# Preparing part of the second layer's weight factors inside that layer, and sending their stores through another engine's queue

## The chip, the cores and the metric

One core of one Trainium2 chip. The metric is the device time of one execution of the program in microseconds (us); the kernel before took 1364.68 us, the median of 3 runs (1362.75 to 1365.15). TensorE is called PE, VectorE DVE, ScalarE ACT, GpSimd POOL and SyncE SP, as in the profile.

## The reference

Softmax attention in chunks of 64 tokens, then a gated layer, then a mixture of four experts, all in float32:

```python
x = attention(q, k, v)                      # 2304 tokens x 512
x = ((x @ w_a) * (x @ w_b)) @ w_out         # 512 -> 1536 -> 512
p = probs / (probs.sum(-1) + 1e-9)
for e in range(4):                          # w1: 512 x 1024, w2: 1024 x 512
    out += p[:, e] * (relu(x @ w1[e]) @ w2[e])
```

## The kernel before, in words

A product of float32 matrices is made of three reduced-precision ones: each factor is cut into a high part (a cast on ACT, `split_hi`, L96) and a low part (the rest, a subtraction on DVE, L103, or on POOL, L111). PE multiplies high by high, high by low and low by high.

**Order of the work.** Everything is in a hand-written schedule: each engine's and each DMA queue's instructions run in the order in which the program issues them. The 2304 tokens are five blocks; block 0 has 256 tokens, the others 512. First the attention is interleaved with the first two slices of the gated layer (the loop over `spans` from L1035, rounds r = 0 to 10); then the loop over F from L1063 does the rest of the gated layer, block by block (`j`; "A" stands for blocks 1 and 2 in one, done in seven products in place of eight). Together this is called the first layer here. From L1155 on comes the mixture, called the second layer: 16 pairs of weight slices g, for blocks 1 and 2 in a first pass (a = 0 to 15) and for blocks 3 and 4 in a second pass (a = 16 to 31), again by seven products. Step s of the loop at L1164 interleaves seven part steps i: the up product of pair a = s (`a_steps`, L619) and the down product of pair o = s - 1 (`o_step`, L850). Block 0 is too small for that and goes along in plain products, `a0_step` (L459 to L461) and `o0_step` (L924), in the steps that `blk0` picks: pairs 0 to 7 in the first pass, pairs 8 to 15 in the second.

**The factors of the second layer.** The seven products need sums of quarters of the weights as well as the quarters. `prep_ahead` makes them: for each of 32 halves n of a pair, a raw tile is loaded (L194, SP's queue); `ent` splits the first two factors out of it (k = 0, 1), `sums` replaces its quarters by sums with four DVE instructions (L103, `raw<-raw`), and `ent` splits the other two (k = 2, 3). Each finished factor, 512 KB of high and low part, is stored to DRAM by `save` (L176, SP's queue, `kept<-w`) and loaded again by `load_l2` (L241, SP's queue, `w<-kept`) when the second layer needs it, once for each pass. That is 32 loads, 128 factors and 128 stores, in a list `ahead` of 160 entries, of which each call of `prep` runs the next one. Before the change the low parts go to POOL and DVE in turn:

```python
t = split_w(half, eng=(nc.gpsimd, nc.vector)[made[0] % 2])
unsaved.append(((g, 4 * i + k), t))
save(1)
```

All 160 entries are run in the first layer: in rounds r > 3 behind every odd step, and later behind six steps of a block and nine of "A".

**Buffers.** A factor's tile comes from the pool `w` (9 tiles), which also holds the first layer's own split weights; a tile is given again when its last reader is done, which for a factor is its store. Raw tiles come from the pool `raw` (4 tiles), which also takes the first layer's weights as they are loaded (L133). In the first layer ACT also casts the gated product (`gh`, L96) whose low part POOL makes (`ag`, L111); both go into PE's next product (L459 to L461). In the second layer ACT and POOL split the up product's results (`hB`) and their differences (`hT`, L830 and L111), which PE reads in the down product.

Of the kernel before, what the change touches and what calls it, by code (L numbers as in the profile page):

```python
# [8 lines left out]
F32 = mybir.dt.float32  # L9
F32R = mybir.dt.float32r  # L10
# [7 lines left out]
P = 128  # L18
# [10 lines left out]
def fused_kernel(  # L29
# [25 lines left out]
    nc = tc.nc  # L55
# [5 lines left out]
    NG2 = w2p.shape[0]  # L61
# [11 lines left out]
    raw_p = ctx.enter_context(tc.tile_pool(name="raw", bufs=4))  # L73
# [9 lines left out]
    late = {}  # L83
# [76 lines left out]
    def w_tile():  # L160
        return w_p.tile([P, 2, 512], F32R, tag="w", name="w")

    def split_w(src, t=None, eng=nc.gpsimd):
        t = w_tile() if t is None else t
        split_hi(t[:, 0, :], src)
        sub_hi(eng, t[:, 1, :], src, t[:, 0, :])
        return t

    saved = {}
    unsaved = []  # L170

    def save(behind=0):
        while len(unsaved) > behind:
            key, t = unsaved.pop(0)
            saved[key] = tc.dram_tile([P, 2, 512], F32, name="kept" + "_".join(map(str, key)))
            nc.sync.dma_start(out=saved[key], in_=t.bitcast(F32))  # L176

    PAIRS = (
        (("A11", "A12"), ("A22", "A21"), ("S2", "S4"), ("S1", "S3")),
        (("A11", "A21"), ("A12", "A22"), ("S2", "S3"), ("S4", "S1")),  # L180
    )
    made = [0]

    def prep_ahead():

        raw2 = {}
        todo = [(g, i) for g in range(NG2) for i in range(2)]

        def load(n):
            if n < len(todo):  # L190
                g, i = todo[n]
                r = raw2[n] = raw_p.tile([P, 1024], F32, tag="raw", name="raw2")
                src = w2p[g, :, 2 * i : 2 * i + 2, :]
                nc.sync.dma_start(out=r, in_=src.rearrange("p a n -> p (a n)"))  # L194

        def ent(n, k):
            g, i = todo[n]
            if n == 0 and k == 0:
                load(0)
            if k == 0:  # L200
                load(n + 1)
            half = raw2[n][:, 512 * (k % 2) :][:, :512]
            made[0] += 1
            t = split_w(half, eng=(nc.gpsimd, nc.vector)[made[0] % 2])
            unsaved.append(((g, 4 * i + k), t))
            save(1)

        def sums(n):
            q = [raw2[n][:, 256 * x : 256 * x + 256] for x in range(4)]
            a11, a12, a22, a21 = q if todo[n][1] == 0 else (q[0], q[2], q[3], q[1])  # L210
            add_sb(a22, a21, a22)
            add_sb(a21, a11, a21, ALU.subtract)
            add_sb(a11, a22, a11, ALU.subtract)
            add_sb(a12, a12, a11, ALU.subtract)

        for n in range(len(todo)):
            yield from (lambda n=n, k=k: ent(n, k) for k in range(2))
            yield lambda n=n: sums(n)
            yield from (lambda n=n, k=k: ent(n, k) for k in (2, 3))

    ahead = list(prep_ahead())

    def prep(n=1):
# [744 lines left out]
    with tc.manual_schedule():  # L968
# [66 lines left out]
        for r, (f, j, i0, nt) in enumerate(spans):  # L1035
            steps = list(ab_steps(f, j, i0, nt))
            for i, go in enumerate(x2):
                steps.insert(2 * i + 2, go)
            fs = (f,) if j < 3 else (0, 1)
            x2 = x2_steps(fs, j, i0, nt) if f or j < 3 else []  # L1040
            slots = slots_by[r] - slot_no[0]
            done = 0
            for i, step in enumerate(steps):
                while done < slots and done * len(steps) <= i * slots:
                    attn_slot()
                    done += 1
                step()
                if done == slots:
                    x_lo_rest()
                if r > 3 and i % 2:  # L1050
                    prep()
                for go in T.get((r, i), ()):
                    go()
            if r == 3:
                domain_probs()
            if r == 9:
                probs_rows()
            if r == 8:
                early.close()
                late["mid"] = mid.enter_context(tc.tile_pool(name="mid", bufs=1, side="right"))  # L1060


        for F in range(1, NP1):  # L1063
            T = {}
            end = F == NP1 - 1
# [20 lines left out]
            if not end:  # L1086
                n = F + 1
# [26 lines left out]
            for j in ("A", 3, 4, 0) if end else (1, 2, 3, 4, 0) if F == 1 else (4, "A", 3, 0):  # L1114
                if j == "A":
                    steps = seq_ab(F)
                    after = [4, 5, 6, 7]
                else:
                    nt = blocks[j][1]
                    s0, s1 = (list(ab_steps(f, j, 0, nt)) for f in (2 * F, 2 * F + 1))  # L1120
                    steps = s0[:4] + s1[:4] + s0[4:] + s1[4:]
                    if len(x2) > 4:
                        after = [6 + i for i in range(8)]
                    elif j == 0:
                        after = [8 + 2 * i for i in range(4)]
                    elif F > 1 and j == 4 and not end:
                        after = [8 + i for i in range(4)]
                    elif j == 1:
                        after = [4 + i for i in range(4)]
                    else:  # L1130
                        after = [5 + i for i in range(4)]
                if end and j == 3:
                    place = dict(B11="s1", B21="s2", T3="s3", T2="s4", T1="s5", T4="s6", B22="s7")
                    for (u, s), go in zip(at, in_turn(in_place(acc[1], acc[2])), strict=True):
                        put(u, s, go)
                for s, step in enumerate(steps):
                    step()
                    for i, go in enumerate(x2):
                        if after[i] == s:
                            go()  # L1140
                    if s in ((0, 1, 2, 3, 4, 5, 6, 7, 8) if j == "A" else (1, 2, 3, 4, 6, 8)):
                        prep()
                    if end and j == 0 and s == 2:
                        assert not ahead
                        save()
                        load_l2(3)
                    for go in T.get((j, s), ()):
                        go()
                fs = (2 * F, 2 * F + 1)
                x2 = [x for i in ((1, 2) if j == "A" else (j,)) for x in x2_steps(fs, i, 0, blocks[i][1])]  # L1150
                if end and j == "A":
                    mid.close()
                    late["1"] = ctx.enter_context(tc.tile_pool(name="late1", bufs=1, side="right"))


        last = 2 * NG2 - 1
# [2 lines left out]
        tmp = []  # L1159

        def blk0(a):
            return 0 <= a <= last and (a < NG2) == (a % NG2 < NG2 // 2)

        for s in range(last + 2):  # L1164
            a, o = s, s - 1
# [50 lines left out]
            for i in range(7):  # L1216
                if a <= last:
                    steps[i]()
                if s == 0 and i in (2, 3):
                    for go in x2[2 * i - 4 : 2 * i - 2]:  # L1220
                        go()
                    if i == 3:
                        first.close()
                        late["2"] = ctx.enter_context(tc.tile_pool(name="late2", bufs=1))
                        late["ps"] = ctx.enter_context(
                            tc.tile_pool(name="po", bufs=2, space=bass.MemoryType.PSUM)
                        )
                if o >= 0:
                    o_step(o, order[i], True if o == last and i == 6 else None)
                    if i < len(ts):  # L1230
                        ts[i]()
                    if o == last:
                        if i == 2:
                            e[0]()
                        if i == 3:
                            e[1]()
                        if i == 4:
                            e[2]()
                            e[3]()
                        if i == 5:  # L1240
                            e[4]()
                            e[6]()
                            e[5]()
                        if i == 6:
                            out_dma(1, "A22", 1, 0)
                for go in more.get(i, ()):
                    go()
                if i == 2 and o >= 0 and blk0(o):
                    o0_step(o)
                if s and i in (2, 5) and blk0(a):  # L1250
                    a0_step(a, i // 3)
                if s == 0 and i == 6:
                    a0_step(0, 0)
                    a0_step(0, 1)
                load_l2(take[i])


_OUTS = [((2304, 512), "float32")]
# [60 lines left out]
```

## Time and profile before

| | us |
|---|---|
| three runs, median (lowest, highest) | 1364.68 (1362.75, 1365.15) |
| the profiled execution's own time | 1359.91 |
| its span, first to last instruction | 1358.1 |
| PE, DVE, POOL, ACT busy in it | 1246.6, 994.0, 805.3, 431.4 |
| mean granted clock of PE | 0.964 |

The span is what the profile covers. Busy is the time in which an engine had at least one instruction of the program running; an idle engine is only of interest where it holds up the one that sets the pace. The granted clock is a share of PE's full speed of 2.4 GHz; at every moment it is at one of two levels, 2.4 or 1.2 GHz, so a mean of 0.92 is a mixture of the two.

### The profile page before, as it was taken

What the parts mean: (1) busy time and instruction counts of PE and PEld (TensorE: products, weight loads), DVE (VectorE), ACT (ScalarE), POOL (GpSimd) and SP (SyncE); (2) the same over time, 40 slices, a digit from 0 to 9 for tenths busy, and PEclk for the clock granted to TensorE, in tenths of its full rate; (3) what the DMA queues carried; (4) which work ended last, traced back from release to release, by engine and by line L of the source; (5) the groups of instructions that cost most, each with busy time, mean ns of one, the idle gap of its engine ahead of it and who ended that gap; (6) DMA issues with size and microseconds to landing.
All of it is one profiled execution on the core that took longest, in us unless ns stands there. A gap on an engine that the chain in (4) does not pass through costs nothing.

```text
span 1358.1 us, 18139 instructions
## 1 busy us (share of the span) xinstructions
PE 1246.6 (92%) x6676; PEld 1018.1 (75%) x6676; DVE 994.0 (73%) x1311; ACT 431.4 (32%) x785; POOL 805.3 (59%) x605
## 2 busy tenths in 40 slices
PE   8986869879889898799999999999999999999996
PEld 5865657667767677688888888887778888888884
DVE  7866457887678776855477677787887787767668
ACT  4643352433343443323421222222342222222211
POOL 4533356665455664635655556779988776655553
PEclk9988888889999999899999999999999999999999
DMA  7675565465465754425455456766567765645452
GB/s 276 213 266 179 188 196 203 159 217 192 165 247 171 234 199 155 171 78 176 153 179 190 157 184 207 231 222 216 194 217 256 244 226 190 200 154 175 167 170 78
DMA packets 76819, 261.34 MB, mean 192 GB/s; under 512 B 8546, under 2 KB 8618, under 8 KB 76732
## 3 DMA queue, kind: packets, MB, share of 16 engines
q1 hardware_dynamic: 76732, 260.19, 56.9%
q8 instruction: 53, 0.87, 0.3%
q14 instruction: 34, 0.28, 0.1%
HBM read 188.29 MB, written 71.86 MB: 192 GB/s over the span
## 4 chain that ended last, share of the span: by engine, by line
PE 56%; DVE 6%; POOL 6%; DMA 3%; issue 3%; ACT 1%; SPq 0%; DVEq 0%; POOLq 0%; ACTq 0%
PE pm L619 22%; PE po L850 20%; PE po L924 3%; PE pm L506 3%; DMA kept<-w 3%; DVE raw L103 2%; POOL hT L111 1%; PE ps L459 1%; PE ps L460 1%; PE ps L461 1%; PE pm L461 1%; PE pm L460 1%; PE pm L459 1%; POOL w L111 1%; POOL hB L111 1%
## 5 line engine op out<-in xcount | busy, mean ns | idle before, releaser
L99 DVE TENSOR_TENSOR y<-po,y 128x1024 f32<-128x1024 f32 x209 | 255.1, 1220 | 94.1 <-PE po L850 94.1
L850 PE MATMUL po<-hT,w 128*128 128x512 f32 x768 | 197.6, 391 | 9.8 <-POOL hT L111 7.4
L619 PE MATMUL pm<-cT,w 128*128 128x512 f32 x768 | 195.9, 390 | 0.0
L619 PE MATMUL pm<-cB,w 128*128 128x512 f32 x672 | 176.6, 399 | 18.6 <-ACT ag L644 18.6
L850 PEld LDWEIGHTS po<-hT,w 128*128 128x128 f32 x768 | 143.2, 188 | 43.9 <-POOL hT L111 11.5
L619 PEld LDWEIGHTS pm<-cT,w 128*128 128x128 f32 x768 | 143.1, 188 | 30.0
L619 PEld LDWEIGHTS pm<-cB,w 128*128 128x128 f32 x672 | 127.0, 192 | 47.4 <-ACT ag L644 20.6
L850 PE MATMUL po<-hB,w 128*128 128x512 f32 x576 | 149.1, 395 | 0.0
L506 PE MATMUL pm<-xh,w 128*128 128x512 f32 (+1 forms) x576 | 141.6, 368 | 2.9 <-DVE ag L99 2.9
L111 POOL TENSOR_TENSOR w<-raw,w 128x512 fp32r<-128x512 f32 x64 | 89.7, 1402 | 86.8 <-ACT w L96 82.9
L459 PE MATMUL ps<-ag,w 128*128 128x512 f32 (+1 forms) x244 | 97.1, 398 | 43.1 <-POOL ag L111 33.5
L850 PEld LDWEIGHTS po<-hB,w 128*128 128x128 f32 x576 | 108.5, 189 | 25.1 <-DVE y L99 0.4
L111 POOL TENSOR_TENSOR ag<-ag,gh 128x512 fp32r<-128x512 f32 (+1 forms) x61 | 77.1, 1268 | 81.1 <-ACT gh L96 73.6
L96 ACT CAST w<-raw 128x512 fp32r<-128x512 f32 x128 | 77.4, 619 | 143.4 <-DMA kept<-w 69.3
L506 PEld LDWEIGHTS pm<-xh,w 128*128 128x128 f32 x576 | 103.6, 197 | 21.4 <-issue 3.3
L103 DVE SCALAR_TENSOR_TENSOR raw<-raw 128x256 f32<-128x256 f32 x128 | 76.3, 596 | 55.3 <-POOL w L111 52.0
L103 DVE SCALAR_TENSOR_TENSOR w<-raw,w 128x512 fp32r<-128x512 f32 x64 | 60.5, 947 | 63.7 <-ACT w L96 62.3
L154 POOL TENSOR_TENSOR t<-t,raw 128x512 int32<-128x512 int32 x36 | 48.0, 1333 | 83.4 <-DVE t L146 26.4
L461 PE MATMUL ps<-gh,w 128*128 128x512 f32 (+1 forms) x244 | 93.6, 384 | 1.1 <-POOL w L111 1.1
L460 PE MATMUL ps<-gh,w 128*128 128x512 f32 (+1 forms) x244 | 93.9, 385 | 0.0
L111 POOL TENSOR_TENSOR hT<-u,hT 128x512 fp32r<-128x512 f32 x64 | 93.4, 1459 | 0.1
L459 PEld LDWEIGHTS ps<-ag,w 128*128 128x128 f32 x244 | 48.7, 199 | 59.5 <-POOL ag L111 39.8
(140 smaller groups left out, 2358.1 us busy)
## 6 DMA issues: line engine op xcount, KB each, us to landing
w<-kept SPq DMA_DIRECT2D x256, 512.0 KB, 4.2
kept<-w SPq DMA_DIRECT2D x128, 512.0 KB, 5.2
raw<-in_w1p_dram SPq DMA_DIRECT2D x36, 512.0 KB, 4.3
raw<-in_w2p_dram SPq DMA_DIRECT2D x32, 512.0 KB, 4.8
q<-in_q_dram SPq DMA_DIRECT2D x18, 256.0 KB, 4.1
k<-in_k_dram SPq DMA_DIRECT2D x18, 256.0 KB, 4.4
v<-in_v_dram SPq DMA_DIRECT2D x18, 256.0 KB, 5.2
pb<-probs_n SPq DMA_DIRECT2D x8, 512.0 KB, 6.9
```

What stands on the lines that cost most here:

```text
L96: nc.scalar.copy(out=dst, in_=src)
L99: nc.vector.tensor_tensor(out=out, in0=in0, in1=in1, op=op)
L103: nc.vector.scalar_tensor_tensor(out=out, in0=in0, scalar=1.0, in1=in1, op0=ALU.mult, op1=op)
L111: eng.tensor_tensor(out=dst, in0=src, in1=hi.bitcast(F32), op=ALU.subtract)
L154: nc.gpsimd.tensor_tensor(out=t.bitcast(I32), in0=t.bitcast(I32), in1=low.bitcast(I32), op=ALU.add)
L459: nc.tensor.matmul(out=ps[:, :n], lhsT=wh, rhs=al, start=(m == 0), stop=False)
L460: nc.tensor.matmul(out=ps[:, :n], lhsT=wh, rhs=ah, start=False, stop=False)
L461: nc.tensor.matmul(out=ps[:, :n], lhsT=wl, rhs=ah, start=False, stop=(m == last))
L506: nc.tensor.matmul(out=st[i][:, :n], lhsT=x, rhs=y, start=m == 0, stop=m == 3 * KD - 1)
L619: nc.tensor.matmul(out=ps, lhsT=x, rhs=y, start=first and kk == 0 and m == 0, stop=kk == 1 and m == 2, skip_group_check=not first,)
L850: nc.tensor.matmul(out=ps[:, d, :], lhsT=x[:, s], rhs=y, start=m == 0, stop=m == 2)
L924: nc.tensor.matmul(out=ps[:, k, :], lhsT=x[:, f, s], rhs=y, start=f == 0 and m == 0, stop=f == 1 and m == 2,)
```

## The change

Stores go out on ACT's queue; low parts are always made on POOL; the order in `prep_ahead` is such that a half's sums stand behind the last two factors of the half before; `prep` is called less often in the first layer and, new, in the second layer's steps s >= 1 at i = 0, 1, 3, 4 and 6, where a factor's tile comes from the pool `raw`; and block 0 goes along in all 16 steps of the first pass and in none of the second.

```diff
-            nc.sync.dma_start(out=saved[key], in_=t.bitcast(F32))
+            nc.scalar.dma_start(out=saved[key], in_=t.bitcast(F32))
...
         def ent(n, k):
             g, i = todo[n]
-            if n == 0 and k == 0:
-                load(0)
-            if k == 0:
-                load(n + 1)
+            save()
             half = raw2[n][:, 512 * (k % 2) :][:, :512]
-            made[0] += 1
-            t = split_w(half, eng=(nc.gpsimd, nc.vector)[made[0] % 2])
+            t = None
+            if "2" in late:
+                t = raw_p.tile([P, 2, 512], F32R, tag="raw", name="made")
+            t = split_w(half, t)
             unsaved.append(((g, 4 * i + k), t))
-            save(1)
+            if k == 3:
+                load(n + 2)
...
-        for n in range(len(todo)):
-            yield from (lambda n=n, k=k: ent(n, k) for k in range(2))
-            yield lambda n=n: sums(n)
-            yield from (lambda n=n, k=k: ent(n, k) for k in (2, 3))
+        yield lambda: (load(0), load(1))
+        for n in range(len(todo) + 1):
+            if n < len(todo):
+                yield from (lambda n=n, k=k: ent(n, k) for k in range(2))
+            if n:
+                yield from (lambda n=n, k=k: ent(n - 1, k) for k in (2, 3))
+            if n < len(todo):
+                yield lambda n=n: sums(n)
...
-                if r > 3 and i % 2:
+                if r > 4 and i % 8 in (1, 4, 6):
                     prep()
...
-                    if s in ((0, 1, 2, 3, 4, 5, 6, 7, 8) if j == "A" else (1, 2, 3, 4, 6, 8)):
+                    if s in ((0, 2, 4, 6, 8, 10) if j == "A" else (1, 3, 6, 9)) and not (end and j == 0):
                         prep()
                     if end and j == 0 and s == 2:
-                        assert not ahead
                         save()
                         load_l2(3)
...
         def blk0(a):
-            return 0 <= a <= last and (a < NG2) == (a % NG2 < NG2 // 2)
+            return 0 <= a < NG2
...
+                if s and i not in (2, 5):
+                    prep()
                 if i == 2 and o >= 0 and blk0(o):
                     o0_step(o)
...
                 load_l2(take[i])
+            if not ahead:
+                save()
```

## Rows read from the trace of the kernel before

**Rows 1.** Windows: us, busy us (and instructions) of PE, PEld, DVE, ACT, POOL; clock; DMA.

```profile
74.00:581.00 507.00, 424.25 (x2124) 340.11 (x2123) 363.60 (x553) 202.37 (x370) 274.21 (x202) 0.92 0.57 194
...
400.00:450.00 50.00, 47.99 (x220) 39.35 (x219) 38.58 (x56) 18.13 (x33) 27.02 (x20) 0.97 0.55 182
350.00:400.00 50.00, 43.87 (x214) 36.49 (x214) 35.04 (x58) 21.51 (x40) 29.43 (x23) 0.95 0.59 209
...
625.00:821.00 196.00, 196.00 (x961) 165.54 (x961) 129.38 (x153) 49.36 (x90) 111.73 (x89) 1.00 0.53 177
...
925.00:1025.00 100.00, 92.49 (x387) 72.82 (x387) 85.01 (x79) 35.27 (x51) 92.26 (x57) 0.98 0.64 215
1025.00:1142.00 117.00, 117.00 (x514) 96.19 (x514) 92.21 (x98) 27.22 (x48) 88.44 (x68) 1.00 0.71 234
```

**Rows 2.** Waits of PE, 74 to 581 us: total us, times, longest us.

```profile
PE ps L459 <- POOL ag L111: 32.4, 15, 7.4
PE pm L619 <- ACT ag L644: 18.6, 4, 6.4
```

**Rows 3.** The chain that ended last, 336 to 581 us: shares of it by line.

```profile
by line: DMA kept<-w 15.6%; issue 12.3%; PE pm L619 9.8%; DVE raw L103 8.7%; PE pm L506 6.9%; POOL w L111 5.1%; DVE xacc L99 4.0%; PE ps L459 3.7%; PE ps L460 3.6%; PE ps L461 3.5%; ACT w L96 3.5%; DVE t L143 2.8%; DVE w L103 2.5%; POOL t L
```

**Rows 4.** Waits of SP's queue, of ACT and of DVE, 74 to 581 us.

```profile
SPq L176 <- DVE w L103: 140.4, 31, 13.5
...
SPq L176 <- POOL w L111: 48.7, 20, 6.6
...
ACT w L96 <- DMA kept<-w: 81.0, 29, 8.3
ACT w L96 <- DVE raw L103: 37.5, 11, 4.6
...
DVE raw L103 <- POOL w L111: 52.0, 22, 6.0
```

**Rows 5.** Groups of instructions, 74 to 581 us: busy us, mean ns, idle before.

```profile
L111 POOL TENSOR_TENSOR w<-raw,w 128x512 fp32r<-128x512 f32 x64 | 89.7, 1402 | 86.8 <-ACT w L96 82.9 <-DVE s L103 2.1 <-PE ps L461 1.8
L96 ACT CAST w<-raw 128x512 fp32r<-128x512 f32 x128 | 77.4, 619 | 143.4 <-DMA kept<-w 69.3 <-DVE raw L103 37.5 <-issue 21.8
L103 DVE SCALAR_TENSOR_TENSOR raw<-raw 128x256 f32<-128x256 f32 x128 | 76.3, 596 | 55.3 <-POOL w L111 52.0
L103 DVE SCALAR_TENSOR_TENSOR w<-raw,w 128x512 fp32r<-128x512 f32 x64 | 60.5, 947 | 63.7 <-ACT w L96 62.3 <-DMA kept<-w 1.3
```

**Rows 6.** Tile views of raw and kept: ns min/median/max; landing in us.

```profile
L103 DVE SCALAR_TENSOR_TENSOR w<-raw,w x64: 674/693/1805, 74.9 to 578.1; 128x512 fp32r<-128x512 f32 x64
L111 POOL TENSOR_TENSOR w<-raw,w x64: 1258/1294/2369, 75.4 to 579.3; 128x512 fp32r<-128x512 f32 x64
...
L176 SPq DMA_DIRECT2D kept<-w x128: 319/382/1330, 75.6 to 581.0; - x128
...
DMA to landing us min/median/max: 2.6/4.4/8.4
```

**Rows 7.** Timeline of the second layer: POOL's low parts and PE's first use.

```profile
742.39 1.29 POOL L111 TENSOR_TENSOR hT<-g,hT 128x512 fp32r<-128x512 f32 x1
...
753.26 1.52 PE L850 MATMUL po<-hT,w 128*128 128x512 f32 x6
...
759.58 1.30 POOL L111 TENSOR_TENSOR hT<-u,hT 128x512 fp32r<-128x512 f32 x1
...
762.88 1.52 PE L850 MATMUL po<-hT,w 128*128 128x512 f32 x6
```

**Rows 8.** Timeline, DVE: once a step, with block 0, then two steps without.

```profile
746.56 0.69 DVE L808 SCALAR_TENSOR_TENSOR g<-pm,pb 128x512 f32<-128x512 f32 x1 [0.16 <-PE pm L619]
771.38 0.69 DVE L808 SCALAR_TENSOR_TENSOR g<-pm,pb 128x512 f32<-128x512 f32 x1 [0.16 <-PE pm L619]
...
1065.70 0.69 DVE L808 SCALAR_TENSOR_TENSOR g<-pm,pb 128x512 f32<-128x512 f32 x1 [0.16 <-PE pm L619]
...
1084.87 0.69 DVE L808 SCALAR_TENSOR_TENSOR g<-pm,pb 128x512 f32<-128x512 f32 x1 [0.16 <-PE pm L619]
```

More of the change, by code (lines that the diff above doesn't have):

```diff
@@ L181, in fused_kernel @@
     )
-    made = [0]
     def prep_ahead():
```

## The prediction, made before the changed kernel was run

> **What bounds the kernel now.** I read the windows first, by stage. In the second layer PE is busy without a gap: 196.0 of 196 us with block 0 in the steps (625 to 821), and 117.0 of 117 without it (1025 to 1142), at clock 1.00 [rows 1]. Only from 925 to 1025, where quarters of blocks 3 and 4 are split beside steps without block 0, is it idle for 7.5 us. The stretch in which factors are prepared is another matter: from 74 to 581 us PE is busy for 424.25 of 507 us, so idle for 82.8, and its clock is 0.92 on average. With two levels, 0.92 means that 16% of the stretch, some 81 us, ran at the low one. If PE worked in it as much as elsewhere (84%), the loss is half of 81 x 0.84 = 34 us. So this stretch holds about 83 + 34 = 117 us over what PE needs, 390 us.
>
> Next the waits of PE there [rows 2]. It waits for low parts from POOL (32.4 us) and for ACT's copies (18.6). But neither engine is full: POOL is busy for 274 of 507 us, DVE for 364, ACT for 202 [rows 1]. So the question is what they wait for. The chain of the second half of this stretch says it [rows 3]: of 245 us, 15.6% are landings of stored factors, 8.7% the in-place sums, 5.1% and 2.5% the low parts on POOL and DVE, 3.5% the casts, together 35.4% or 87 us. The matmuls named there have 27%. The loop "cast, low part, store, landing, tile free, next cast" is the pace for long stretches. The waits show its joints [rows 4]. ACT stands 81.0 us before a cast until a store has landed, 37.5 until the sums are done; DVE stands 52.0 us before the sums until POOL has read the raw tile; SP's queue stands 140.4 + 48.7 us at the stores, with loads behind. All engines work in order, so a cast that waits holds up the copy or gated product behind it, and PE waits for that.
>
> **The change, part by part.**
>
> *Fewer factors in the first layer.* Counting the calls of prep: rounds 5 to 10 make 22, F = 1 makes 20, F = 2 to 4 make 18 each, F = 5 makes 14; 110 of now 161 entries, against all 160. These are 87 factors and 22 sums; 41 factors and 10 sums move. ACT loses 41 x 0.62 = 25 us of casts there, DVE 40 x 0.60 = 24 us of sums [rows 5].
>
> *Low parts on POOL.* DVE loses 64 of 0.95 us, 60.5 us; POOL makes 87 in place of 64, 23 x 1.40 = 32 us more [rows 5]. DVE would come to 364 - 85 = 279 us and POOL to 306 us, of a stretch that is still above 390: neither full.
>
> The same low part costs 0.69 us on DVE and 1.29 on POOL by the medians, with maxima of 1.81 and 2.37, about one instruction of the other engine more [rows 6]: the two at times take turns. The Trainium skill (SBUF — State Buffer, "Who interferes with whom") says that a DVE instruction with two inputs in SBUF and a POOL instruction that reads SBUF exclude each other for their whole length; the maxima agree. By that rule the two engines' changes would be one sum, as in the first rival.
>
> *Stores on ACT's queue.* SP no longer stands at stores, so its loads go out when their tiles are free. ACT instead waits for the low part of the factor before. That entry is two or three steps old, so I cost the wait at nothing as long as POOL's backlog is shorter than that; behind the wait on ACT stand the copies and casts of the gated product. The issue itself has no row on ACT: nothing at least, 0.38 us by SP's median and 1.33 at most [rows 6]. At the median 87 of them are 33 us of ACT's 305 idle ones. The landing of 4.4 us stays; with calls further apart it should mostly end before the tile is wanted.
>
> *Sums later.* Two other entries now stand between the low parts and the sums, and between the sums and the casts of their results, so the 52.0 and 37.5 us of waits [rows 4] should nearly go. The next raw load goes on SP behind the last low part of its tile, as it did.
>
> *The sum for the first layer.* Unknown is how much of 117 us goes. The calm end is 400 to 450 us, where factors are made too: idle 2.0 us and clock 0.97, a loss of 3.3 in 50, or 7%. With that everywhere, 390 / 0.93 = 419, a gain of 88. The other end is 350 to 400: idle 6.1, clock 0.95, loss 8.2, 16%: 390 / 0.84 = 464, a gain of 43. That end is itself one of the better stretches, so I go down to a quarter of the 117, 29. I take 58: half of the loss, and two thirds of the 87 us that the chain runs through preparation.
>
> *The second layer's first pass.* A step with block 0 takes 771.38 - 746.56 = 24.8 us, one without 1084.87 - 1065.70 = 19.2 [rows 8]. Block 0 moves eight times 5.6 = 45 us of PE from one pass to the other, which is nothing in sum; steps without it keep PE busy in the second pass already [rows 1]. Four factors a step add 4 x 1.29 = 5.2 us to POOL, which has 111.7 of 196 us, 14.1 in a step: 19.3 of 24.8. ACT gets 2.5 us and four issues, DVE 4 x 0.60, SP nine raw loads whose wait is short, with the factors' loads queued behind. Is a difference's low part late then? The first ends at 743.68 and is read at 753.26, 9.6 us of slack; the fourth ends at 760.88 and is read at 762.88, 2.0 us [rows 7]. The entries at i = 0 and 1 fall where there is much slack, those at 3 and 4 before and behind the fourth one's cast, while POOL has gaps. Between nothing and 12 us (one 1.3 us low part in the way in nine of ten steps); I take 3. In return block 0 now covers steps 12 to 15, where over half of the 7.5 us idle lies: -4 (-6 to 0). Stores add 41 x 512 KB; a DMA share of 0.71 is borne without a gap at 1025 to 1142 [rows 1].
>
> *The end.* The last step loses block 0 as cover; at worst its 5.6 us, at best a gain of 2, I take 0.
>
> Sum: -58 + 3 - 4 = -59 from the profiled execution's 1359.9 us, 1301. The median of the runs is 4.8 us higher: **1306 us**. Bounds: -88 - 6 - 2 = -96, or 1269; -29 + 12 + 5.6 = -11, or 1353.
>
> **The rivals.**
>
> *DVE and POOL take turns and become the pace.* Then -85 on DVE and +32 on POOL are one sum, at the medians -64 x 0.69 - 40 x 0.60 + 23 x 1.29 = -38 us [rows 5, 6]; with -1 behind it the time is 1364.7 - 39 = 1326. For it: low parts of mean 1.40 against a median of 1.29. Against: both together are not the chain's largest part. The Trainium skill's rule on the two engines, above, would have it so.
>
> *Store landings stay in the loop.* Tiles of w are still short, the 15.6% of 245 us = 38 us of landings stay, and the gain falls to 58 x (87 - 38) / 87 = 33: 1332. For it: the landing itself does not change, and the wait for the tile is ACT's largest. The Trainium skill (DMA: Bandwidth & Descriptors, "Issuing engines are not separate DMA queues") says that issuing from several engines saves only the sequencer's time to initiate, as all run on the same DMA engines. By that alone moving the stores would give 128 x 0.38 us of an SP that is not the pace. SP's 189 us of waits at stores speak for more.
>
> *ACT is held, slower.* In the second layer a factor's cast waits for its tile of the pool raw until the store two entries before has landed: 4.4 us. At i = 6, 0 and 1 the entries follow in 2.7 us (24.8 less block 0's 5.6, over 7). If such waits reach the casts of the differences, they decide from 2.0 us on, the fourth one's slack: 2.4 us over in eleven steps is 26 us, and if ACT's stores also eat the first layer's gain, 1391. Against it: behind i = 6, 0 and 1 stands slack of up to 9.6 us.
>
> *It does nothing:* the conversions of the first layer's own weights, not the factors, set the pace once the loop is loosened: 1365.
>
> **How the numbers follow.** My forecast has 0.55, turns on DVE and POOL 0.15, landings 0.12, ACT held 0.12, nothing 0.06. The first three give faster, less a little for their upper edges: 0.81. Same (within 0.2%, about what a measurement of this kernel can tell from no change) 0.06, slower 0.13. The range is 1269 to 1353: the first three cases, 8 in 10.
>
> **What would show it.** From 74 us to the second layer's start: PE idle under 50 us, clock above 0.94, waits "sums for POOL" and "cast for sums" nearly gone, ACT's wait for landings under 40 us. The second layer's first pass takes about 16 x 24.8 us with no PE wait of note, and the second 16 x 19.2. I am wrong if PE's wait for POOL's `ag` or ACT's copies stays above 45 us, if ACT shows long waits before its own stores, or if the first pass's steps grow beyond 25.5 us.

## The result and the profile after

The changed kernel takes 1311.62 us, the median of 4 runs (1309.49 to 1317.45), beside 1364.45 us of the kernel before. The ratio is 0.9621 with a 95% interval of 0.9587 to 0.9656: 53 us faster. The forecast was 1306 in a range of 1269 to 1353.

First the windows of the profile after: the first layer's stretch with preparation, the second layer's first pass, and the two stretches up to the first product's scaling of the second layer, of after and (a row not shown yet) of before.

```profile
74.00:546.00 472.00, 427.03 (x2216) 344.69 (x2215) 334.48 (x454) 183.59 (x332) 307.08 (x227) 0.96 0.44 154
...
590.00:865.00 275.00, 268.65 (x1287) 222.12 (x1286) 221.01 (x248) 83.12 (x154) 206.06 (x159) 1.00 0.73 259
...
74.00:574.00 500.00, 455.03 (x2365) 368.91 (x2364) 352.83 (x478) 193.77 (x347) 318.21 (x234) 0.96 0.44 157
```

```profile
74.00:629.00 555.00, 472.25 (x2358) 380.74 (x2357) 390.49 (x584) 215.31 (x389) 288.67 (x211) 0.92 0.55 187
```

PE's idle time in the first layer falls from 82.8 us [rows 1] to 45.0, and the clock rises from 0.92 to 0.96. Between the two longer stretches (555 and 500 us) that is 38 us of idle time and 17 us of busy time (472.25 against 455.03 us, for about as many matmuls). Two other columns matter later: DVE is busy for 38 us less up to the second layer, where 85 were expected, and POOL for 30 us more.

The waits after, from 74 to 550 us (PE, ACT, DVE, SP's queue):

```profile
PE ps L461 <- POOL ag L111: 20.1, 12, 6.0
PE pm L621 <- ACT ag L646: 15.5, 4, 6.8
...
ACT w L96 <- DMA raw<-in_w2p_dram: 57.3, 13, 8.3
ACT w L96 <- POOL w L111: 56.6, 29, 6.5
...
ACT w L96 <- DMA kept<-w: 6.3, 5, 2.9
...
DVE raw L103 <- POOL w L111: 8.9, 2, 6.8
...
SPq L192 <- POOL w L111: 133.3, 19, 16.4
```

Beside rows 4 the old joints are nearly gone: ACT's wait for stores 81.0 to 6.3 us, DVE's before the sums 52.0 to 8.9. In their place ACT waits 56.6 us for POOL ahead of its own stores, and 57.3 us for raw loads, which SP now issues late, behind POOL. Before, that wait was next to nothing (74 to 581 us):

```profile
ACT w L96 <- DMA raw<-in_w2p_dram: 2.1, 1, 2.1
```

It comes with the new order of the entries: a half's load now stands two entries ahead of its first cast, where it stood five ahead. It is tempting to read the gain from the old joints that are gone; the experiments say otherwise.

The second layer pays in the stretch where factors are made. PE's waits from 591 to 850 us, ACT's in the whole first pass (590 to 865), then two steps of DVE's timeline:

```profile
PE po L852 <- DVE y L99: 5.9, 10, 0.8
```

```profile
ACT made L96 <- DMA kept<-made: 60.9, 16, 6.4
```

```profile
643.13 0.69 DVE L810 SCALAR_TENSOR_TENSOR g<-pm,pb 128x512 f32<-128x512 f32 x1 [0.16 <-PE pm L621]
656.33 3.60 DVE L103 SCALAR_TENSOR_TENSOR raw<-raw 128x256 f32<-128x256 f32 x4
669.35 0.69 DVE L810 SCALAR_TENSOR_TENSOR g<-pm,pb 128x512 f32<-128x512 f32 x1 [0.16 <-PE pm L621]
```

A step takes 26.2 us there instead of 24.8 [rows 8]. The four sums of a step take 3.6 us of DVE in place of the 4 x 0.6 expected, and the accumulation `y` behind them comes late once a step. PE's waits for it are 5.9 of the 10 us by which ten steps are longer; no wait shows the rest. The long sums alone do not make `y` late, as e1 will show. ACT's cast does wait for the store two entries before (60.9 us), the mechanism of the rival "ACT is held", while PE waits for ACT for only 0.2 us in this stretch.

The step marker of these lines (DVE's scaling `g`, once a step) cuts every profile into three parts. "First layer" is the time of the first marker; it differs between two profiles of the changed kernel by 6.5 us, so smaller differences there say nothing. "Steps 1 to 10" runs from the second marker to the twelfth, "rest" from the twelfth to the end of the span. Step 0, between the first two markers (17.5 to 19.7 us), is in no column. The ratio is to the kernel before as it was timed with each group of runs, with medians of 1360.5 to 1364.5 us.

| kernel | median us | ratio to before (95%) | first layer | steps 1 to 10 | rest |
|---|---|---|---|---|---|
| before | 1364.5 | 1 | 629.7 | 233.9 | 476.9 |
| changed | 1311.6 | 0.9621 (0.9587 to 0.9656) | 574.0 | 258.2 | 457.9 |
| changed, again (e7) | 1315.2 | 0.9636 (0.9609 to 0.9663) | 580.5 | 256.2 | 458.0 |
| e1, stores on SP | 1302.6 | 0.9559 (0.9533 to 0.9584) | 573.7 | 252.0 | 457.9 |
| e2, sums first | 1303.2 | 0.9563 (0.9536 to 0.9590) | 572.8 | 255.1 | 457.9 |
| e3, low parts in turn | 1309.0 | 0.9610 (0.9588 to 0.9632) | 577.4 | 252.7 | 457.5 |
| e4, all in the first layer | 1427.5 | 1.0476 (1.0451 to 1.0502) | 698.1 | 233.9 | 477.2 |
| e5, pace and block 0 only | 1297.3 | 0.9509 (0.9495 to 0.9523) | 566.5 | 254.2 | 457.9 |
| e6, e1 and e2 together | 1298.7 | 0.9525 (0.9507 to 0.9542) | 568.6 | 252.2 | 457.9 |
| e8, e4 with stores on SP | 1383.7 | 1.0139 (1.0122 to 1.0157) | 653.2 | 233.9 | 477.4 |
| f1, e5 with block 0 divided | 1312.4 | 0.9628 (0.9591 to 0.9665) | 566.8 | 248.7 | 476.1 |
| f2, 70 entries in the second | 1311.8 | 0.9632 (0.9592 to 0.9672) | 558.1 | 270.8 | 458.7 |
| f3, 79 entries | 1322.5 | 0.9705 (0.9683 to 0.9728) | 555.3 | 291.2 | 457.3 |
| f4, 58 entries | 1309.6 | 0.9619 (0.9594 to 0.9644) | 562.7 | 267.3 | 457.7 |

Block 0's eight moved shares (45 us) stand in the first pass where it is not divided, so steps and rest are compared among kernels that place it alike.

### The profile page after: what moved, and what is told of

Read it like the earlier page. It is cut to its first block, busy times and chain, and to the rows that moved or that the text cites. A ratio compares the mean times of both kernels' runs of the same rounds, so it can differ in the third digit from the quotient of the medians.

```text
span 1307.7 us, 18028 instructions
## 1 busy us (share of the span) xinstructions
PE 1230.7 (94%) x6674; PEld 1004.6 (77%) x6676; DVE 993.0 (76%) x1247; ACT 432.2 (33%) x785; POOL 889.2 (68%) x669
## 4 chain that ended last, share of the span: by engine, by line
PE 48%; DVE 15%; POOL 3%; issue 2%; ACT 2%; DMA 1%; DVEq 0%; ACTq 0%; POOLq 0%
PE pm L621 19%; PE po L852 18%; PE po L926 3%; DVE raw L103 3%; DVE y L99 3%; PE pm L508 2%; DVE u L810 2%; POOL w L111 1%; DMA raw<-in_w2p_dram 1%; PE ps L461 1%; PE ps L463 1%; PE ps L462 1%; DVE u L99 1%; PE pm L463 1%; PE pm L462 1%
## 5 line engine op out<-in xcount | busy, mean ns | idle before, releaser
L111 POOL TENSOR_TENSOR w<-raw,w 128x512 fp32r<-128x512 f32 x87 | 121.8, 1400 | 77.1 <-ACT w L96 71.8
L508 PE MATMUL pm<-xh,w 128*128 128x512 f32 (+1 forms) x576 | 135.8, 357 | 0.0
L103 DVE SCALAR_TENSOR_TENSOR raw<-raw 128x256 f32<-128x256 f32 x128 | 113.2, 885 | 12.2 <-POOL w L111 8.9
L508 PEld LDWEIGHTS pm<-xh,w 128*128 128x128 f32 x576 | 99.7, 190 | 16.6
L99 DVE TENSOR_TENSOR xacc<-ps,xacc 128x512 f32<-128x512 f32 (+1 forms) x112 | 68.0, 628 | 40.8 <-PE ps L463 40.4
L96 ACT CAST w<-raw 128x512 fp32r<-128x512 f32 x87 | 53.9, 620 | 130.7 <-DMA raw<-in_w2p_dram 57.3
L463 PE MATMUL ps<-gh,w 128*128 128x512 f32 (+1 forms) x244 | 92.0, 377 | 0.5 <-POOL w L111 0.5
L462 PE MATMUL ps<-gh,w 128*128 128x512 f32 (+1 forms) x244 | 92.0, 377 | 0.0
L832 POOL TENSOR_TENSOR u<-m,u 128x512 f32<-128x512 f32 x62 | 82.6, 1331 | 2.4
```

The source lines that it names most:

```text
L96: nc.scalar.copy(out=dst, in_=src)
L99: nc.vector.tensor_tensor(out=out, in0=in0, in1=in1, op=op)
L103: nc.vector.scalar_tensor_tensor(out=out, in0=in0, scalar=1.0, in1=in1, op0=ALU.mult, op1=op)
L111: eng.tensor_tensor(out=dst, in0=src, in1=hi.bitcast(F32), op=ALU.subtract)
L462: nc.tensor.matmul(out=ps[:, :n], lhsT=wh, rhs=ah, start=False, stop=False)
L463: nc.tensor.matmul(out=ps[:, :n], lhsT=wl, rhs=ah, start=False, stop=(m == last))
```

## The experiments

The theory at first was that of the prediction: the loop of preparation is the pace, and its joints (SP at the stores, the sums between a half's factors) hold it up. Each part of the change was undone alone.

**e1, stores on SP's queue.**

```diff
-            nc.scalar.dma_start(out=saved[key], in_=t.bitcast(F32))
+            nc.sync.dma_start(out=saved[key], in_=t.bitcast(F32))
```

> The changed kernel (1311.6 us) with the stores back on SP's queue, all else as changed. Theory (the loop of preparation was the pace; SP stood 189 us at stores, with loads behind them): SP stands at stores again, at least 60 us from 74 to 546 us, raw loads come later, ACT's wait for raw loads grows from 57 us to 70 or more, and the time rises by 5 to 20 us, 1317 to 1332. Rival (the queue saves only the time of issuing): 1309 to 1315, the same within the interval.

1302.6 us: neither, but faster. SP stands at stores again, 155.7 us, and ACT waits for a store's landing for 27.7 us in place of 6.3, yet the first layer ends at the same time. ACT's wait for raw loads did not grow either (58.0 us). The difference in its profile lies in steps 1 to 10, 252.0 against 258.2 and 256.2 us. Two groups of DVE's instructions in these steps, of the changed kernel (591.6 to 849.8 us) and then of e1 (591.3 to 843.3): busy us, mean ns, idle before.

```profile
L103 DVE SCALAR_TENSOR_TENSOR raw<-raw 128x256 f32<-128x256 f32 x40 | 36.9, 922 | 1.0
L810 DVE SCALAR_TENSOR_TENSOR m<-m,pb 128x512 f32<-128x512 f32 x10 | 13.8, 1383 | 0.3
```

```profile
L103 DVE SCALAR_TENSOR_TENSOR raw<-raw 128x256 f32<-128x256 f32 x40 | 36.0, 899 | 1.0
L810 DVE SCALAR_TENSOR_TENSOR m<-m,pb 128x512 f32<-128x512 f32 x10 | 8.3, 834 | 0.3
```

The sums are as long in e1, but the scaling `m<-m,pb` just ahead of them is 5.5 us shorter in sum, and PE's waits for `y` fall from 5.9 to 0.8 us. In the changed kernel POOL's low part of a factor falls beside that scaling:

```profile
653.42 1.30 POOL L111 TENSOR_TENSOR made<-raw,made 128x512 fp32r<-128x512 f32 x1
653.49 1.78 DVE L810 SCALAR_TENSOR_TENSOR m<-m,pb 128x512 f32<-128x512 f32 x1
```

In e1's step at that time this low part ends at 652.18 us, before the scaling starts (652.78), which then takes 0.69 us. e7, the changed kernel once more, lies between in both: 11.5 us of scaling, steps of 256.2. So the stores on ACT's queue cost 4 to 6 us here by what they shift; the rest of e1's 9 us no profile places. The queue of stores was no joint that held up PE.

**e2, the sums between a half's own factors.**

```diff
-        for n in range(len(todo) + 1):
...
+        for n in range(len(todo)):
+            yield from (lambda n=n, k=k: ent(n, k) for k in range(2))
+            yield lambda n=n: sums(n)
+            yield from (lambda n=n, k=k: ent(n, k) for k in (2, 3))
```

> The changed kernel with the sums of a half again between its own second and third factor, all else as changed. Theory (the joints of the loop): the waits 'DVE sums for POOL' and 'ACT cast for sums' come back with 20 us or more each from 74 to 546 us, and the time rises by 12 to 25 us, 1324 to 1337. Rival (fewer entries in the first layer are what counts, the joints are then covered): 1309 to 1316.

The waits came back as foretold (ACT and DVE, 74 to 546 us):

```profile
ACT w L96 <- DVE raw L103: 42.5, 14, 5.0
...
DVE raw L103 <- POOL w L111: 49.9, 13, 7.1
```

The time did not: 1303.2 us, not 1324 to 1337. Some 80 us of waits that the change had taken away were not on the path at this pace. With this order ACT's wait for raw loads is gone again (1.5 us in place of 57.3).

**e3, low parts on POOL and DVE in turn.**

```diff
-            t = split_w(half, t)
+            made[0] += 1
+            t = split_w(half, t, (nc.gpsimd, nc.vector)[made[0] % 2])
```

> The changed kernel with the low parts made on POOL and DVE in turn again, in both layers. Theory (DVE and POOL take turns, so moving a low part to POOL lengthens the shared time by 0.6 us each): the mean of an in-place sum falls from 0.885 us to under 0.75, the second layer's first ten steps come down from 25.8 to 25.2 us or less, and the time is 0 to 10 us shorter, 1301 to 1312. Rival (a lighter DVE is what the change lives on): 64 low parts of 0.69 to 0.95 us on DVE again cost 15 to 40 us, 1327 to 1350.

1309.0 us, in the first theory's range and within the interval of the changed kernel. The mean of a sum fell only from 0.885 to 0.804 us, so the sizes were too hopeful, but the lighter DVE is not what the change lives on.

**e4, all factors in the first layer.** The old calls of `prep` and the old division of block 0, the other three parts as changed:

```diff
-                if r > 4 and i % 8 in (1, 4, 6):
+                if r > 3 and i % 2:
...
-                    if s in ((0, 2, 4, 6, 8, 10) if j == "A" else (1, 3, 6, 9)) and not (end and j == 0):
+                    if s in ((0, 1, 2, 3, 4, 5, 6, 7, 8) if j == "A" else (1, 2, 3, 4, 6, 8)):
...
-            return 0 <= a < NG2
+            return 0 <= a <= last and (a < NG2) == (a % NG2 < NG2 // 2)
```

> The changed kernel with all factors made in the first layer at the old pace of calls and block 0 divided over the passes as before; stores on ACT, later sums and low parts on POOL stay. Theory (a third fewer entries carry a good part of the gain): the first layer, to the first product's scaling of the second, grows from 574 us by 25 to 45 us, the second layer's first pass loses its 10 us of longer steps, and the time is 1328 to 1350. Rival (the joints alone give the gain): the first layer grows by under 12 us and the time is 1305 to 1318.

1427.5 us, some 65 us slower than the kernel before: the first layer grows by 124 us and not by 25 to 45, so the pace is worth far more, and at the old pace the other three parts do harm. ACT's waits from 74 to 546 us:

```profile
ACT w L96 <- DMA raw<-in_w2p_dram: 121.5, 21, 8.8
ACT w L96 <- POOL w L111: 96.3, 51, 7.1
```

And ACT, its queue and POOL in a part of the timeline (start, duration, what, idle before):

```profile
338.21 0.33 ACTq L176 DMA_DIRECT2D kept<-w  x1
338.58 0.62 ACT L96 CAST w<-raw 128x512 fp32r<-128x512 f32 x1 [3.41 <-POOL w L111]
...
339.28 1.29 POOL L111 TENSOR_TENSOR w<-raw,w 128x512 fp32r<-128x512 f32 x1 [1.10 <-ACT w L96]
...
340.60 0.33 ACTq L176 DMA_DIRECT2D kept<-w  x1
340.97 0.62 ACT L96 CAST w<-raw 128x512 fp32r<-128x512 f32 x1 [1.28 <-POOL w L111]
...
341.67 1.29 POOL L111 TENSOR_TENSOR w<-raw,w 128x512 fp32r<-128x512 f32 x1 [1.10 <-ACT w L96]
...
342.99 0.33 ACTq L176 DMA_DIRECT2D kept<-w  x1
```

The store stands on the engine that makes the next cast, and waits for POOL's low part of the last factor. So ACT and POOL run in a ring of 2.4 us a factor, each idle while the other works, and ACT's casts and copies of the gated product stand behind it. PE's longest wait in that window is for POOL's `ag`, 54.5 us.

The theory was changed: the pace alone gives the gain, and the other three parts give nothing or cost. A second group tried that, beside the changed kernel once more.

**e5, the pace alone.** The kernel before with the calls, the tile from `raw` and block 0 as changed, so that "pace" here takes in the place of block 0:

```diff
-            t = split_w(half, eng=(nc.gpsimd, nc.vector)[made[0] % 2])
+            t = None
+            if "2" in late:
+                t = raw_p.tile([P, 2, 512], F32R, tag="raw", name="made")
+            t = split_w(half, t, (nc.gpsimd, nc.vector)[made[0] % 2])
...
-                if r > 3 and i % 2:
+                if r > 4 and i % 8 in (1, 4, 6):
...
-            return 0 <= a <= last and (a < NG2) == (a % NG2 < NG2 // 2)
+            return 0 <= a < NG2
...
+                if s and i not in (2, 5):
+                    prep()
```

> The kernel before with only the new pace: as many calls in the first layer and as many in the second as the changed kernel, block 0 all in the first pass, a factor's tile from the pool raw there; stores on SP, sums between a half's own factors and low parts on POOL and DVE in turn stay as before. Theory (the pace gives the whole gain and the other three parts give nothing or cost a little): the first layer ends at 574 us or up to 6 us earlier, the second layer's first ten steps take 248 to 254 us, and the time is 1292 to 1306. Rival (the parts need each other, the joints of the old loop come back): the first layer ends at 585 to 605 us, the time is 1315 to 1335.

1297.3 us, 0.9509 of the kernel before: the pace gives 66 us, and the rest of the change takes some 14 to 18 of them back. The old joints are all there; SP stands at stores (74 to 546 us) nearly as long as the 189 us of rows 4:

```profile
SPq L176 <- DVE w L103: 126.9, 22, 11.3
SPq L176 <- POOL w L111: 56.3, 16, 13.1
```

PE's longest waits in e5's whole span:

```profile
PE ps L462 <- POOL ag L111: 23.7, 16, 3.6
PE pm L622 <- ACT ag L647: 8.7, 4, 4.4
PE po L853 <- POOL hT L111: 7.5, 7, 1.4
PE pm L622 <- DVE gh L99: 4.8, 2, 4.1
PE po L853 <- DVE y L99: 4.2, 6, 1.3
```

**e6, e1 and e2 together.** The edits of both, low parts all on POOL.

> The changed kernel with stores on SP's queue and the sums between a half's own factors again; low parts all on POOL, new pace. Theory (each of the two costs by itself, the queue 6 us in the second layer, the later sums 3 us there and 1 in the first): 1292 to 1300. Rival (both costs are the same one, ACT held behind POOL): 1300 to 1306, no better than either alone.

1298.7 us: what the two edits give back adds up, about 9 and 8 us alone and 13 to 17 together. Beside e5 it also says that low parts all on POOL cost nothing measurable (0.9525 against 0.9509, intervals that overlap; e5 also has the old places of the raw loads).

**e7, the changed kernel once more.**

> The changed kernel once more, beside the others of this group, so that differences of some us between them are read on one chip. By all theories 1305 to 1317, a ratio to the kernel before of 0.958 to 0.966.

1315.2 us, as expected; e5 and e6 of the same group are clear of it.

**e8, e4 with stores on SP's queue.** The edit of e1 on e4.

> The kernel of e4 (all factors in the first layer at the old pace, 1427.5 us) with the stores on SP's queue. Theory (ACT, which issues the store, stands behind POOL's low part of the factor before, so that at the old pace ACT and POOL go in a ring of some 2.4 us a factor): ACT's waits for POOL's low parts go from 96 us to under 25 us from 74 to 546 us, and the time falls to 1350 to 1390. Rival (128 low parts on POOL are too much whatever the queue): 1410 to 1430.

1383.7 us, 44 us less than e4: with ACT free of the stores its waits for POOL's low parts no longer stand among its long ones, and the ring is gone. Still 19 us slower than the kernel before: at the old pace, later sums, the later raw loads that come with them and 128 low parts on POOL cost as well; which of them was not tried. ACT waits 134.0 us for raw loads there, its longest wait, against 2.1 before.

**f1, e5 with block 0 divided as before.**

```diff
-            return 0 <= a < NG2
+            return 0 <= a <= last and (a < NG2) == (a % NG2 < NG2 // 2)
```

> The kernel of e5 (new pace alone, 1297.3 us) with block 0 divided over the two passes as in the kernel before. Theory (block 0 is needed as cover for the factors made in the second layer and for the split of blocks 3 and 4): the first layer ends as in e5, at 566 us, but steps 8 to 16 of the second layer, now without block 0, are 8 to 18 us longer in sum than 19.2 us each, against 2 us in e5 over 24.8, and the time is 1303 to 1315. Rival (the moved block is free of effect, its PE time is the same anywhere): 1295 to 1301.

1312.4 us, 15 more than e5, all behind the first layer (566.8 against 566.5). PE's wait for the differences' low parts, 584 to 1010 us, f1 and then e5:

```profile
PE po L853 <- POOL hT L111: 16.6, 12, 3.5
```

```profile
PE po L853 <- POOL hT L111: 6.5, 6, 1.4
```

Block 0's products are the cover under which POOL makes factors and splits blocks 3 and 4. Without them as cover 51 of e5's 66 us remain.

**f2, f3 and f4, more entries in the second layer.** f2 calls prep at (1, 4, 8) of a block and (0, 2, 5, 7, 10) of "A" and at every i but 2 of a step (90 and 70 entries); f3 thins further, to 81, and calls it at every i; f4 keeps e5's calls but for "A", (0, 3, 6, 9), so 102 and 58.

> The kernel of e5 with 90 entries in the first layer and 70 in the second (six a step at i other than 2) in place of 110 and 50. Theory (each entry in the first layer costs what the 50 moved ones gave back, 63 us over 50 or 1.26 us, and 0.13 us in the second): the first layer's end moves from 566.5 to about 541 us, the first steps grow by under 8 us in sum, and the time is 1274 to 1290. Rival (the loop is no longer the pace at 110, so fewer entries give nothing): the first layer's end stays over 558 us and the time is 1292 to 1310.

> The kernel of e5 with 81 entries in the first layer and 79 in the second, seven a step. Theory (1.26 us an entry): the first layer ends at about 530 us, the second layer's first eleven steps pay 5 to 20 us more than in e5, and the time is 1268 to 1292. Rival (the second layer's engines are full at seven a step: ACT behind the stores, POOL and DVE in turn): steps of 27 us and more, and a time of 1298 to 1325.

> The kernel of e5 with four calls in place of six in 'A' (F = 2 to 5): 102 entries in the first layer and 58 in the second, still five a step, now up to step 12. Theory (at five a step a moved entry costs 0.13 us in the second layer, and from 110 to 90 entries the first layer gave back 8.4 us over 20, 0.42 us an entry): the first layer ends at 563 us, the first twelve steps pay 1 us more, and the time is 1292 to 1297. Rival (the calls taken out of 'A' were not the ones that hurt): the first layer ends at 566 us or later, 1296 to 1303.

All three were slower than e5: 1311.8, 1322.5 and 1309.6 us. In the first layer the return falls off: from 160 entries to 110 it ends 63 us earlier, from 110 to 90 only 8, little more than the 6.5 us by which two profiles of one kernel differ, and from 90 to 81 only 3, which is less. In the second layer ten steps with six or seven a step take 17 and 37 us more than with five; there the entries also fall elsewhere in a step, and no run separates their number from their place. f4 shows something else, as it also has five a step: PE's wait from 582 to 850 us, and then f4's timeline of DVE:

```profile
PE po L927 <- DVE y L99: 14.2, 10, 3.5
```

```profile
685.60 3.74 DVE L103 SCALAR_TENSOR_TENSOR raw<-raw 128x256 f32<-128x256 f32 x4
691.58 0.68 DVE L811 SCALAR_TENSOR_TENSOR g<-pm,pb 128x512 f32<-128x512 f32 x1
```

A half has five entries and a step five calls, so the sums fall at the same i in every step. With 110 entries ahead they fall 8.7 us behind the marker in e5 (i = 3) and 13.2 us behind it in the changed kernel (i = 4); with 102 they fall 6.0 us ahead of it (i = 0), and block 0's down product waits for DVE in nearly every step, 1.4 us on average and 3.5 at most. e5's timeline of DVE:

```profile
661.00 0.68 DVE L811 SCALAR_TENSOR_TENSOR g<-pm,pb 128x512 f32<-128x512 f32 x1
669.72 1.80 DVE L103 SCALAR_TENSOR_TENSOR raw<-raw 128x256 f32<-128x256 f32 x4
```

The same number of entries a step thus costs 6 us (254.2 - 10 x 24.8) or 19 us (267.3), by where they stand. PE's wait of 14.2 us is about the whole difference, and it stands behind the sums; the other entries are shifted with them, which no run takes apart. The best version found is e5, with e6 level with it.

## Why the prediction was right, and where it was not

- **What bounds the kernel: right.** In the first layer the loop of preparation set the pace. Of the 117 us to be had, 49 to 56 came back in the first layer by the two profiles' markers; 58 was taken.
- **The step that failed: which part gives it.** The prediction put the gain down to the joints, SP at the stores (189 us) and the waits around the sums (52.0 and 37.5). e1 and e2 put these joints back at the new pace and got 8 to 9 us faster. The number of entries in a given stretch is what counts: e5 has the old joints and 66 us of gain. A wait in rows 4 was a sign that the loop had no slack; that the same waits cover each other once a third of the entries is gone is argued from these times and not shown by itself. What the joints alone would give at the old pace, with the low parts and the loads as before, no run shows.
- **The sum came out near partly by luck.** For the first layer the pace by itself gives 63 us (e5), and the other parts took 8 to 14 of them back where the prediction had them give. 58 was half of a loss, whichever part was to give it, and so hides both errors.
- **DVE's relief was mis-sized.** Expected were -85 us on DVE and +32 on POOL up to the second layer; measured are -38 and +30. About 24 of the missing 47 us are the sums: 88 of them take as long as 128 did before, with a mean of 0.868 us in place of 0.596 [rows 5]. Most of the rest lies in other instructions of the first layer that are longer too (those on its own weights, L142 and L143, by 12 us, the sums `s` by 7). POOL's greater share alone does not make the sums long: e2, with the old order and all low parts on POOL, has a mean of 0.600 us up to the second layer. Nor does the old order alone keep them short (0.750 in e5). This is the term of the first rival, in which DVE and POOL take turns; it came out larger than the rival's -38 in sum, -8. The Trainium skill (SBUF — State Buffer, "Who interferes with whom") has it that such instructions exclude each other; the longer sums agree. As the pace it did not matter: e3 is within the changed kernel's interval. The sums after the change, 74 to 574 us:

```profile
L103 DVE SCALAR_TENSOR_TENSOR raw<-raw 128x256 f32<-128x256 f32 x88 | 76.4, 868 | 11.2 <-POOL w L111 8.9
```

- **Sums later: the raw load was put at nothing.** "As it did" was wrong: the new order brings the load nearer to its first cast, and ACT's wait for raw loads went from 2.1 to 57.3 us. e2 undoes it together with the sums' place and is 8 us faster; the two are not told apart.
- **Stores on ACT's queue: the price was not nothing.** The issue is cheap, 0.326 us by the tile view of `kept`, near SP's 0.319 at least [rows 6]. The wait ahead of it, costed at nothing, is 56.6 us on ACT from 74 to 550. In the first layer e1's profile shows no loss by it at the new pace; in the second, e1's steps 1 to 10 are 4 to 6 us shorter. The Trainium skill (DMA: Bandwidth & Descriptors, "Issuing engines are not separate DMA queues") promises only the issuing time from another queue; the time that came of it is below even that, as the issuing engine was one with work behind it. On the landing the measurement differs from that sentence, and from the prediction's "stays": it is 2.6 us in the changed kernel's first layer against 5.0 in e1. The 4.4 us of rows 6 are a median over stores and loads together; for the stores alone it was 5.2.
- **The second layer's first pass: within its bounds, by another way.** 3 us were taken of 0 to 12; measured are 258.2 - 248 = 10 (8 in e7). The low parts of the differences, of which the slack was worked out, were not late; DVE's accumulation was.
- **Block 0: right in sign and in size.** Steps 12 to 15 were given -4 us. The table's last column is 476.9 - 457.9 = 19 us shorter, of which 248 - 233.9 = 14 only moved into steps 1 to 10, so about 5 are gained, the end of the kernel included. f1 shows that without the move the whole of e5 would be 15 us slower, as the new entries need the cover too, a term that the sum had only as "nothing in sum".
- **The sum by the profiles.** -55.7 for the first layer, +10 for steps 1 to 10 and -5 for the rest make the -50.4 us between the two spans; the prediction had -58, +3 and -4.
- **The signs.** PE's idle time (45.0 us), the clock (0.96) and ACT's wait for landings (6.3) came as named, and PE's waits for `ag` and ACT's copies (35.6) stayed under 45. Two signs of being wrong came true as well: ACT's long waits before its own stores, and steps beyond 25.5 us (25.8 on average). Both point at the parts that took time back.
- **The rivals.** Landings staying in the loop fell (81.0 to 6.3 us). "ACT is held" named a mechanism that exists; e4 shows it deciding, not in the second layer but in the first, at the old pace. "It does nothing" fell with the 53 us.

## What to carry to other kernels

When a side loop is the pace, first ask how much of it can run where engines have slack; thinning it was worth 66 us here, 15 of them by cover from block 0, and mending the loop's joints gave nothing at the new pace. A store belongs on a queue whose engine has nothing behind it: on a computing engine, issued ahead of that engine's next work as here, it makes the engine wait for the producer. Issuing it later on ACT was not tried. When calls and a list of entries have the same period, the list's heaviest entry meets the same place each time, so choose that place.

## What the runs showed of the hardware

Four in-place sums on DVE of 128x256 elements took from 1.80 us (e5, nothing of POOL in the way) to 5.51 us (changed kernel, at 475.9 us, beside a row of POOL instructions). These are the latter:

```profile
475.91 5.51 DVE L103 SCALAR_TENSOR_TENSOR raw<-raw 128x256 f32<-128x256 f32 x4
476.79 1.48 POOL L111 TENSOR_TENSOR ag<-ag,gh 128x512 fp32r<-128x512 f32 x1
...
478.24 1.47 POOL L111 TENSOR_TENSOR w<-raw,w 128x512 fp32r<-128x512 f32 x1
...
479.67 1.47 POOL L111 TENSOR_TENSOR w<-t,w 128x512 fp32r<-128x512 f32 x1
```

A median store lands in 2.6 us from ACT's queue in the first layer of the changed kernel, and in 5.0 us from SP's queue in e1, which differs in that queue alone. In the second layer, where the DMA engines' share is 0.73 in place of 0.44, the two are alike (5.9 and 5.8 us). Before, on SP's queue, it was 5.2. The pages of the profiles of before, changed (two lines) and e1:

```profile
kept<-w SPq DMA_DIRECT2D x128, 512.0 KB, 5.2
...
kept<-w ACTq DMA_DIRECT2D x87, 512.0 KB, 2.6
kept<-made ACTq DMA_DIRECT2D x41, 512.0 KB, 5.9
...
kept<-w SPq DMA_DIRECT2D x87, 512.0 KB, 5.0
```

That SP's queue also carries the loads is the likely reason; no run shows it apart. The shorter landing did not shorten the first layer.
